# Where the output product stands between the gate and the val products of a fused attention and GLU kernel

## The chip, the cores and the metric

The kernel runs on one core of a Trainium2 chip. The metric is the time of one execution on the device, in microseconds (us). The core has five engines with a queue each: TensorE (PE in the profile) multiplies matrices, and its weight loads are a row of their own (PEld); VectorE (DVE), ScalarE (ACT) and GpSimd (POOL) work on elements; SyncE (SP) issues transfers. Each engine takes the instructions of its queue in the order in which the program lists them, and waits where an instruction needs what another engine has not finished.

## The reference

Two layers are fused. The first is a cross-covariance attention: for each of 4 batches, with q, k and v of 6016 rows and 256 channels,

```
s = kn.T @ qn / tau          # kn, qn: k and q scaled to length 1 down each column
a = softmax(s)               # 256 x 256
x = v @ a
```

The second is a gated linear unit on the 24064 rows of x, with 1536 hidden units:

```
gate = sigmoid(x @ w_gate)
out  = (gate * (x @ w_val)) @ w_out
```

## The kernel before, in words

The kernel never forms x. For each batch it multiplies the small matrix `a` with the weights, G = a @ w_gate and H = a @ w_val (function `gh`, 12 pieces a batch, each two matmuls of 512 columns and one store), and then needs only v: gate is v @ G, val is v @ H.

*Chunks and slots.* A batch is cut into 12 chunks of 512 rows (the last has 384), and a chunk into 12 slots `f`, one for each 128 hidden units. A slot is the unit in which everything is laid out. In it `glu` (line 655) makes one tile of the hidden layer:

- gate: two matmuls of 512 columns into `ps_gate`, then on ScalarE `g_sb` = tanh(gate/2) (line 676);
- val: two matmuls into `ps_val`;
- on VectorE `hT` = (tanh + 1) x val (line 677), in bf16. The missing factor 1/2 is carried in the scale with which H is stored.

`ps_gate` and `ps_val` have two buffers each, so a slot's val waits for the `hT` of two slots before.

*The output product.* hT @ w_out of a chunk runs during the next chunk. It is done with a scheme of seven block products in place of eight (the tables `PRODUCTS` and `ORDER`), so some of its operands are sums of blocks of hT. Those sums are made by `a_sum` on VectorE: the sum `m` = 0 (line 703, half the size), 1 (line 705) and 2 (line 707), each for two halves of the hidden units. The first half is done in the chunk itself, after the slots 7, 9 and 11 (`OWN_SLOTS`). The second half is done in the next chunk, after the slots 1, 3 and 5 (`NEXT_SLOTS`). `out_work` lists 84 matmuls of 128 columns for a chunk, and `run_work` takes one share of the list in each slot, seven of them (after the 384-row chunk the list is shorter, six in a slot, and sum 0 is first used in slot 2). By the order of the list, the second half of sum 0 is first used in slot 3 (by the first matmul of the share), that of sum 1 in slot 5 (the fifth), and that of sum 2 in slot 7 (the third). When a product of the list is complete, ScalarE copies it out of `ps_o` (`part`, line 756, and `whole`, line 763), and GpSimd adds the pieces (lines 757, 758, 773, 774).

*Side work.* The attention of batch b+1 is prepared during batch b: squares (ScalarE), sums for the scores (VectorE), score matmuls, and at the end of the batch the pieces of G and H. `side_work` writes a table of what follows each slot. The stores of G and H alternate between ScalarE (line 622) and VectorE (line 624). The pieces that do not fit any more go into `spill`, that is into the first slots of the next batch. In the last batch there is no such work.

*The order by hand.* The schedule is manual: the order in the program is the order in each queue. In a slot the main loop lists

```
glu(b, ci, f, ...)                # gate, val, tanh, hT
a_sum(...)                        # in the slots 1, 3, 5: for the chunk before
run_work(work, ...)               # the share of the output product
a_sum(...)                        # in the slots 7, 9, 11: for this chunk
for fn, a in spill + side: fn(*a) # scores, G/H, squares
```

`glu` has a parameter `between`, work that is listed between the gate's and the val's matmuls. Before the change only the very first chunk uses it, for pieces of G and H.

Of the kernel before, what the change touches and what calls it, by code (L numbers as in the profile page):

```python
# [9 lines left out]
FP32 = mybir.dt.float32  # L10
BF16 = mybir.dt.bfloat16
INT32 = mybir.dt.int32
ACT = mybir.ActivationFunctionType
# [36 lines left out]
def kernel(  # L50
# [20 lines left out]
    nc = tc.nc  # L71
    P = nc.NUM_PARTITIONS
# [9 lines left out]
    FC = DFF // P  # L82
# [3 lines left out]
    CH = TPC * P  # L86
# [11 lines left out]
    def pool(name, bufs, **kw):  # L98
        return ctx.enter_context(tc.tile_pool(name=name, bufs=bufs, **kw))
# [10 lines left out]
    gpool = pool("gpool", 3)  # L110
# [13 lines left out]
    def mm(out, lhsT, rhs, start, stop, **kw):  # L124
        nc.tensor.matmul(out, lhsT=lhsT, rhs=rhs, start=start, stop=stop, **kw)  # L125
# [74 lines left out]
    for f0, nf in pieces:  # L200
        if f0 + nf == DFF:
            load_v(0, 1)
        for w, src in enumerate((moe_w_gate, moe_w_val)):
            nc.gpsimd.dma_start(
                out=w_sb[w][f0 // FG][:, :, ds(f0 % FG, nf)],
                in_=src.rearrange("(t p) f -> p t f", p=P)[:, :, ds(f0, nf)],
# [5 lines left out]
    for n in range(FC // TPC):  # L212
        w_f32[n] = f32pool.tile([P, TPC, C], FP32, tag="f32", name="w_f32")
        nc.gpsimd.dma_start(
            out=w_f32[n], in_=moe_w_out.rearrange("(t p) c -> p t c", p=P)[:, n * TPC : (n + 1) * TPC, :]
# [412 lines left out]
    def gh(b, piece, pl, tag, act=None):  # L628
        gh_store(b, piece, gh_mms(b, piece, pl, tag), piece[3] == 0 if act is None else act)
# [25 lines left out]
    def glu(b, ci, f, between=None):  # L655
        t0, nt = groups[ci]
        n = nt * P
        G, H = st[b]["gh"]
        vT = vts[b, ci]
        if f == 0:  # L660
            hts[b, ci] = hpool.tile([P, FC, CH], BF16, tag="hT", name="hT")
        ps_gate = psg.tile([P, CH], FP32, tag="g", name="ps_gate")
        ps_val = psv.tile([P, CH], FP32, tag="v", name="ps_val")
        for ps, w in ((ps_gate, G), (ps_val, H)):
            for ib in range(CB):
                mm(
                    ps[:, :n],
                    w[f // (FG // P)][:, ib, ds(f % (FG // P) * P, P)],
                    vT[:, ib, :nt, :],
                    start=(ib == 0),  # L670
                    stop=(ib == CB - 1),
                )
            if between is not None and w is G:
                between()
        g_sb = gpool.tile([P, CH], FP32, tag="g", name="g_sb")
        nc.scalar.activation(out=g_sb[:, :n], in_=ps_gate[:, :n], func=ACT.Tanh, scale=0.5)  # L676
        nc.vector.scalar_tensor_tensor(  # L677
            out=hts[b, ci][:, f, :n],
            in0=g_sb[:, :n],
            scalar=1.0,  # L680
            in1=ps_val[:, :n],
            op0=ALU.add,
            op1=ALU.mult,
        )
# [3 lines left out]
    def a_sum(b, ci, g, m):  # L688

        nt = groups[ci][1]  # L690
        half = nt // 2
        hT = hts[b, ci]
        if (b, ci, g) not in sums:
            sums[b, ci, g] = spool.tile(
                [P, 5, FC // 4, CH // 2], BF16, tag=f"s{g}", name="sums", bufs=2 - g
            )
        f0, f1 = g * (FC // 2), (g + 1) * (FC // 2)
        n = half * P
        first, count = A_STEPS[m]
        out = sums[b, ci, g][:, first : first + count, :, :n].rearrange("p m j n -> p j m n")  # L700
        x = hT[:, f0:f1, : 2 * n].rearrange("p (j k) (r n) -> p j k r n", k=2, r=2)
        if m == 0:
            nc.vector.tensor_tensor(out=out[:, :, 0], in0=x[:, :, 0, 0], in1=x[:, :, 1, 1], op=ALU.add)  # L703
        elif m == 1:
            nc.vector.tensor_tensor(out=out, in0=x[:, :, 0], in1=x[:, :, 1], op=ALU.add)  # L705
        else:
            nc.vector.tensor_tensor(out=out, in0=x[:, :, :, 0], in1=x[:, :, :, 1], op=ALU.subtract)  # L707
# [94 lines left out]
    def run_work(work, share):  # L802

        upto = sum(w[0] for w in work) * share
        done = 0
        while work and done < upto:
            cost, fn, *args = work.pop(0)
            fn(*args)
            done += cost

    def store():
        while stores:
            b, ci = stores.pop(0)
            t0, nt = groups[ci]
            nc.sync.dma_start(out=out_rows[b][:, t0 : t0 + nt, :], in_=ffn.pop((b, ci))[:, :nt, :])
# [43 lines left out]
    for g, (t0, nt) in enumerate(groups0):  # L859
# [11 lines left out]
        while adds:  # L871
            w, last_sq = adds.pop()
# [55 lines left out]
    def side_work(b):  # L928
# [4 lines left out]
        def at(slot, fn, *a):  # L933
            side.setdefault(divmod(slot, FC), []).append((fn, a))
# [14 lines left out]
        n = b + 1  # L949
# [5 lines left out]
        for g, (t0, nt) in enumerate(groups if b == 0 else []):  # L955
            s0 = first + g * (last - first) // NCH
# [3 lines left out]
            for w in range(2):  # L960
                at(s0 + 1 + 4 * w, narrow_square, n, g, w)
                slot = s0 + 3 + 4 * w
                at(slot + slot % 2, narrow_add, n, g, w)
        step = (last - first) / len(wide)
        for g, (t0, nt) in enumerate(wide if b else []):
            s0 = first + int(g * step)
# [19 lines left out]
        s0 = 8 * FC + 2  # L986
# [27 lines left out]
        at(s0 + 28, all_sums, n)  # L1014
        at(s0 + 28, gh_tiles, n)
        for i, piece in enumerate(gh_order):
            slot = s0 + 30 + 2 * i
            if slot < NCH * FC:
                at(slot, gh, n, piece, *((pss, "s"), (psm, "m"))[i % 2])
            else:  # L1020
                spill.setdefault((n, *divmod(slot - NCH * FC, FC)), []).append((gh, (n, piece, psm, "m")))
# [8 lines left out]
    def gh_pieces(ns):  # L1030
        for n in ns:
            gh(0, gh_first[n], *gh_banks[n % 4])

    prev = None
    for b in range(B):
        side = side_work(b)
        for ci in range(NCH):
            final = (b, ci) == (B - 1, NCH - 1)
            for f in range(FC):
                mid = gh_mid.get(f) if (b, ci) == (0, 0) else None  # L1040
                glu(b, ci, f, None if mid is None else (lambda: gh_pieces(mid)))
                if prev is not None:
                    if f == 4:
                        store()
                    if f + final in NEXT_SLOTS and prev != (0, 0):
                        a_sum(*prev, 1, NEXT_SLOTS[f + final])
                    run_work(work, 1 / max(1, FC - final - f))
                if f in OWN_SLOTS and not final and (b, ci) != (0, 0):
                    a_sum(b, ci, 0, OWN_SLOTS[f])
                for fn, a in spill.get((b, ci, f), []) + side.get((ci, f), []):  # L1050
                    fn(*a)
                if (b, ci) == (0, 0):
                    gh_pieces(gh_end.get(f, ()))
            prev = (b, ci)
            if not final:
                work = out_work(*prev)
# [39 lines left out]
```

## Time and profile before

| | before |
|---|---|
| median of 3 runs | 805.0 us (803.94 to 805.98) |
| span of the profiled run | 803.2 us |
| granted TensorE clock, mean | 0.998 |
| TensorE busy | 779.8 us |
| VectorE busy | 688.5 us |
| ScalarE busy | 526.3 us |
| GpSimd busy | 443.6 us |
| tanh (line 676), 576 times | 588 ns each |
| hT (line 677), 576 times | 672 ns each |
| sums of the lines 703, 705 and 707, 92 times each | 546, 1102 and 1029 ns each |

How to read it: busy time is what an engine spent in instructions other than waits, and the rest of the span is what it stood idle. The mean of a group is over all its instructions, the smaller ones of the 384-row chunks too. The line of every matmul is that of a helper (L125), so matmuls are told apart by the names of their tiles: `ps_gate`, `ps_val`, `ps_o` (output product), `ps_s` (scores), `ps_gh` (G and H). In the timeline a line can stand for several instructions of a kind that follow each other (x7), and then the second number is from the start of the first to the end of the last. The end of a matmul is modelled, so the distance from start to start is what counts.

### The profile page before, as it was taken

How to read it: one execution, taken by the hardware profiler on the slowest of the kernel's cores; microseconds unless marked ns; L12 is line 12 of the kernel's file. 1: busy time of each engine (PE TensorE's matmuls, PEld its weight loads, DVE VectorE, ACT ScalarE, POOL GpSimd, SP SyncE). 2: the span in 40 equal slices, each digit the busy share in tenths (PEclk: the TensorE clock that was granted, in tenths of full speed). 3: DMA queues.
4: the chain of work that ended last, by engine and by line, in shares of the span. 5: the costliest groups of instructions: out<-in, count | busy, mean ns of one | idle time of the engine just before them, and what ended most of it. 6: DMA issues, size and time to landing. Idle time of an engine off the chain costs nothing.

```text
span 803.2 us, 18022 instructions
## 1 busy us (share of the span) xinstructions
PE 779.8 (97%) x6861; PEld 497.7 (62%) x6875; DVE 688.5 (86%) x1044; ACT 526.3 (66%) x891; POOL 443.6 (55%) x621
## 2 busy tenths in 40 slices
PE   3899999999999999999999999999999999999998
PEld 2556666666656666666665666666666566666666
DVE  5767989999878898889988889989987888888886
ACT  3766777766667767676667677766666565665664
POOL 3566565546454677565842755676754344444443
PEclk9999999999999999999999999999999999999999
DMA  9997759432676899863477599987234333432402
GB/s 214 203 199 127 131 97 139 89 66 54 137 146 132 165 173 191 172 123 53 103 138 155 109 172 179 186 152 137 51 71 80 60 66 65 82 67 64 88 29 73
DMA packets 82775, 95.15 MB, mean 118 GB/s; under 512 B 52512, under 2 KB 58528, under 8 KB 82688
## 3 DMA queue, kind: packets, MB, share of 16 engines
q0 software_dynamic: 25616, 55.85, 39.4%
q1 hardware_dynamic: 56496, 37.30, 21.6%
q8 instruction: 53, 0.87, 0.4%
q10 hardware_dynamic: 576, 0.85, 0.3%
q14 instruction: 34, 0.28, 0.1%
HBM read 79.04 MB, written 24.64 MB: 129 GB/s over the span
## 4 chain that ended last, share of the span: by engine, by line
PE 93%; DMA 4%; DVE 1%; issue 1%; ACT 1%; POOL 0%; DVEq 0%; ACTq 0%; POOLq 0%
PE ps_gate L125 30%; PE ps_val L125 30%; PE ps_o L125 27%; DMA qk_sb<-in_k_dram 4%; PE ps_s L125 4%; PE ps_gh L125 2%; DVE hT L677 0%; ACT acc L292 0%; DVE sums L703 0%; ACT g_sb L676 0%; PE ps_end L125 0%; DVE qs L354 0%; DVE sums L705 0%; DVE sums L707 0%; PE ps_n L125 0%
## 5 line engine op out<-in xcount | busy, mean ns | idle before, releaser
L676 ACT ACTIVATE g_sb<-ps_gate 128x512 f32<-128x512 f32 (+1 forms) x576 | 337.9, 588 | 224.5 <-PE ps_gate L125 204.7
L677 DVE SCALAR_TENSOR_TENSOR hT<-g_sb,ps_val 128x512 bf16<-128x512 f32 (+1 forms) x576 | 385.7, 672 | 95.5 <-ACT g_sb L676 77.5
L125 PE MATMUL ps_val<-vT,gh_H 128*128 128x512 bf16 (+1 forms) x1152 | 337.5, 375 | 1.4 <-DVE hT L677 1.4
L125 PE MATMUL ps_gate<-vT,gh_G 128*128 128x512 bf16 (+1 forms) x1152 | 337.6, 375 | 0.2
L125 PEld LDWEIGHTS <-sums 128*128 128x128 bf16 x2670 | 182.8, 98 | 85.2 <-DVE sums L703 3.9
L125 PEld LDWEIGHTS <-gh_H 128*128 128x128 bf16 x1152 | 112.7, 98 | 132.6 <-issue 2.4
L773 POOL TENSOR_TENSOR out_sb<-out_sb,m_sb 128x256 f32<-128x256 f32 x89 | 89.2, 1002 | 170.8 <-ACT out_sb L763 145.6
L125 PE MATMUL ps_o<-w_sums,sums 128*128 128x128 bf16 x1602 | 154.9, 219 | 2.0 <-DVE sums L703 1.9
L125 PEld LDWEIGHTS <-hT 128*128 128x128 bf16 x1200 | 88.2, 98 | 46.9
L757 POOL TENSOR_TENSOR m_sb<-m_sb 128x128 f32<-128x128 f32 x89 | 51.3, 576 | 98.5 <-ACT m_sb L756 98.3
L705 DVE TENSOR_TENSOR sums<-hT 128x1536 bf16<-128x1536 bf16 (+1 forms) x92 | 101.4, 1102 | 0.0
L125 PEld LDWEIGHTS <-gh_G 128*128 128x128 bf16 x1152 | 92.8, 98 | 12.5 <-DVE gh_G L624 0.3
L125 PE MATMUL ps_o<-w_out_sb,sums 128*128 128x128 bf16 x1068 | 96.3, 219 | 0.0
L125 PE MATMUL ps_o<-w_sums,hT 128*128 128x128 bf16 x1068 | 95.5, 219 | 0.0
L707 DVE TENSOR_TENSOR sums<-hT 128x1536 bf16<-128x1536 bf16 (+1 forms) x92 | 94.7, 1029 | 0.0
L758 POOL TENSOR_TENSOR m_sb<-m_sb 128x128 f32<-128x128 f32 x89 | 81.4, 914 | 7.0
L774 POOL TENSOR_TENSOR out_sb<-out_sb 128x256 f32<-128x256 f32 x89 | 78.4, 881 | 7.0
L763 ACT COPY out_sb<-ps_o 128x512 f32<-128x512 f32 x89 | 52.2, 587 | 11.4 <-PE ps_o L125 8.5
L703 DVE TENSOR_TENSOR sums<-hT 128x768 bf16<-128x768 bf16 (+1 forms) x92 | 50.3, 546 | 0.0
L125 PE MATMUL ps_s<-qk_sb 128*128 128x256 bf16 (+1 forms) x194 | 34.7, 297 | 15.4 <-DMA qk_sb<-in_k_dram 8.5
L756 ACT COPY m_sb<-ps_o 128x384 f32<-128x384 f32 x89 | 42.7, 479 | 6.5 <-PE ps_o L125 4.0
L252 ACT ACTIVATE sq<-qk_sb 128x1024 bf16<-128x1024 bf16 (+3 forms) x36 | 35.6, 1009 | 12.0 <-DMA qk_sb<-in_k_dram 11.9
(105 smaller groups left out, 510.0 us busy)
## 6 DMA issues: line engine op xcount, KB each, us to landing
out_dram<-out_sb SPq DMA_DIRECT2D x43, 512.0 KB, 3.4
v_sb<-in_v_dram POOLq DMA_DIRECT2D x44, 256.0 KB, 5.3
acc<-sq POOLq DMA_DIRECT2D x16, 512.0 KB, 7.0
qk_sb<-in_q_dram POOLq DMA_DIRECT2D x14, 512.0 KB, 10.3
qk_sb<-in_k_dram POOLq DMA_DIRECT2D x14, 512.0 KB, 8.2
qs<-qk_sb POOLq DMA_DIRECT2D x20, 256.0 KB, 5.5
qk_sb<-in_q_dram POOLq DMA_DIRECT2D x15, 256.0 KB, 5.6
qk_sb<-in_k_dram POOLq DMA_DIRECT2D x15, 256.0 KB, 6.3
```

The costliest lines, as they stand in the source:

```text
L125: nc.tensor.matmul(out, lhsT=lhsT, rhs=rhs, start=start, stop=stop, **kw)
L676: nc.scalar.activation(out=g_sb[:, :n], in_=ps_gate[:, :n], func=ACT.Tanh, scale=0.5)
L677: nc.vector.scalar_tensor_tensor(out=hts[b, ci][:, f, :n], in0=g_sb[:, :n], scalar=1.0, in1=ps_val[:, :n], op0=ALU.add, op1=ALU.mult,)
L703: nc.vector.tensor_tensor(out=out[:, :, 0], in0=x[:, :, 0, 0], in1=x[:, :, 1, 1], op=ALU.add)
L705: nc.vector.tensor_tensor(out=out, in0=x[:, :, 0], in1=x[:, :, 1], op=ALU.add)
L707: nc.vector.tensor_tensor(out=out, in0=x[:, :, :, 0], in1=x[:, :, :, 1], op=ALU.subtract)
L756: nc.scalar.copy(m, states[p]["ps"][:, : 3 * P].rearrange("p (n c) -> p n c", c=P))
L757: nc.gpsimd.tensor_tensor(out=m[:, 1, :], in0=m[:, 1, :], in1=m[:, 2, :], op=ALU.add)
L758: nc.gpsimd.tensor_tensor(out=m[:, 2, :], in0=m[:, 1, :], in1=m[:, 0, :], op=ALU.add)
L763: nc.scalar.copy(o[:, p : p + half + 1 : half, :], states[p]["ps"].rearrange("p (t c) -> p t c", c=C),)
L773: add(out=ends, in0=ends, in1=states[p]["m"][:, 1:3, :], op=ALU.add)
L774: add(out=ends, in0=ends, in1=mids, op=ALU.subtract)
```

## The change

The share of the output product moves from behind the hidden tile to between its gate and its val products. Tanh is listed ahead of that share, so that ScalarE can work on it while TensorE does output matmuls, and VectorE has both operands of hT when val is done. What stands behind the slot (the sums, the side work) keeps its place. The G/H pieces at the end of a batch move from even slots to the odd slots just before. The first chunk, which has no output product yet, keeps its G/H pieces between gate and val; there too tanh is now listed ahead of them.

```
@@ glu
         ps_val = psv.tile([P, CH], FP32, tag="v", name="ps_val")
+        g_sb = gpool.tile([P, CH], FP32, tag="g", name="g_sb")
         for ps, w in ((ps_gate, G), (ps_val, H)):
             for ib in range(CB):
                 mm(
...
-            if between is not None and w is G:
-                between()
-        g_sb = gpool.tile([P, CH], FP32, tag="g", name="g_sb")
-        nc.scalar.activation(out=g_sb[:, :n], in_=ps_gate[:, :n], func=ACT.Tanh, scale=0.5)
+            if w is G:
+                nc.scalar.activation(out=g_sb[:, :n], in_=ps_gate[:, :n], func=ACT.Tanh, scale=0.5)
+                if between is not None:
+                    between()
         nc.vector.scalar_tensor_tensor(
@@ side_work
         for i, piece in enumerate(gh_order):
-            slot = s0 + 30 + 2 * i
+            slot = s0 + 29 + 2 * i
@@ the main loop
                 mid = gh_mid.get(f) if (b, ci) == (0, 0) else None
-                glu(b, ci, f, None if mid is None else (lambda: gh_pieces(mid)))
+                if prev is not None:
+                    mid = lambda: run_work(work, 1 / max(1, FC - final - f))
+                elif mid is not None:
+                    mid = lambda ns=mid: gh_pieces(ns)
+                glu(b, ci, f, mid)
                 if prev is not None:
                     if f == 4:
                         store()
                     if f + final in NEXT_SLOTS and prev != (0, 0):
                         a_sum(*prev, 1, NEXT_SLOTS[f + final])
-                    run_work(work, 1 / max(1, FC - final - f))
```

## The prediction

> **What bounds the kernel now.** I read the page first: busy shares, slices, the chain that ended last.
>
> ```profile
> PE 779.8 (97%) x6861; PEld 497.7 (62%) x6875; DVE 688.5 (86%) x1044; ACT 526.3 (66%) x891; POOL 443.6 (55%) x621
> ...
> PE 93%; DMA 4%; DVE 1%; issue 1%; ACT 1%; POOL 0%; DVEq 0%; ACTq 0%; POOLq 0%
> ```
>
> TensorE is the bound: 93% of the chain. Its idle time is almost all in the first 37 us, which the change does not touch. So the question is what the change does to the few waits that TensorE has after that, and whether it makes new ones. The view of waits lists the old ones, and what VectorE waits for:
>
> ```profile
> DVE hT L677 <- ACT g_sb L676: 77.5, 161, 1.3
> PEld L125 <- DVE sums L703: 3.9, 7, 1.1
> PE ps_o L125 <- DVE sums L703: 1.9, 2, 1.0
> PE ps_val L125 <- DVE hT L677: 1.4, 3, 0.8
> ```
>
> Columns: total us, times, longest. VectorE waits 77.5 us for tanh, but it is not the bound. TensorE waits for VectorE for some 5 us in all: that is what can be won. Adding up, after 37 us, every gap between matmul starts that is longer than the matmul in front of it needs gives the same 5 us. Last I read the timeline of the last batch, where each chunk repeats the one before and no other work disturbs it (start, duration):
>
> ```profile
> 697.20 0.59 PE L125 MATMUL ps_gate<-vT,gh_G 128*128 128x512 bf16 x2
> 697.63 0.59 PE L125 MATMUL ps_val<-vT,gh_H 128*128 128x512 bf16 x2
> 697.83 0.60 ACT L676 ACTIVATE g_sb<-ps_gate 128x512 f32<-128x512 f32 x1 [0.66 <-PE ps_gate L125]
> 698.46 0.69 DVE L677 SCALAR_TENSOR_TENSOR hT<-g_sb,ps_val 128x512 bf16<-128x512 f32 x1 [0.57 <-ACT g_sb L676]
> 699.06 1.25 DVE L705 TENSOR_TENSOR sums<-hT 128x1536 bf16<-128x1536 bf16 x1
> ...
> 699.70 0.59 PE L125 MATMUL ps_gate<-vT,gh_G 128*128 128x512 bf16 x2
> ...
> 700.62 0.50 PE L125 MATMUL ps_o<-w_out_sb,sums 128*128 128x128 bf16 x6
> ...
> 701.57 1.13 DVE L707 TENSOR_TENSOR sums<-hT 128x1536 bf16<-128x1536 bf16 x1
> ...
> 703.08 0.55 PE L125 MATMUL ps_o<-w_sums,sums 128*128 128x128 bf16 x7
> ```
>
> This is slot 3 to slot 7 of a chunk. Gate and val take 0.43 us each (697.20, 697.63), seven output matmuls 0.39 us, a slot 1.25 us. The hT product waits for tanh, and starts 1.26 us after the gate. The sum of slot 3 ends at 700.31 and is first needed by the fourth of the six matmuls at 700.62, that is at 700.79 (0.056 each). The sum of slot 5 ends at 702.70 and is needed by the third of the seven at 703.08, that is at 703.19. What a wait costs at least is seen where one happened:
>
> ```profile
> 234.09 0.35 DVE L703 TENSOR_TENSOR sums<-hT 128x384 bf16<-128x384 bf16 x1
> ...
> 234.50 0.34 PE L125 MATMUL ps_o<-w_sums,sums 128*128 128x128 bf16 x3 [0.97 <-DVE sums L703]
> ```
>
> The sum ends at 234.44 and TensorE goes on at 234.50: 0.06 us. So the slack of the two sums above is 700.79 - 700.31 - 0.06 = 0.42 us and 703.19 - 702.70 - 0.06 = 0.43 us.
>
> **What the Trainium skill says.** "TensorE: Matmul & The Clock Gate", section "Wait — 56ns, not 53.3ns?", gives 55.6 ns and 215.7 ns from start to start for 128 and 512 columns; this trace has 56 and 215, so TensorE is at its rate, and an order of matmuls can only gain by removing waits. The same page, section "Architectural detail: the array is 16× 32×32, not 1× 128×128", says that TensorE may pull weight loads ahead of matmuls but that ScalarE and VectorE are strict queues. In this trace a weight load starts one matmul early and no more, so a load that waits for sums holds all that is behind it. "SBUF — State Buffer", section "SBUF: two separate sides", says VectorE and GpSimd exclude each other on a shared port for some operations. The trace fits in part: L705 takes 0.95 us in some chunks and 1.25 in the one above, where GpSimd's adds lie beside it.
>
> **The change, part by part.**
>
> *Output share between gate and val.* No matmul is added or removed. On TensorE the order "gate, val, output, side" becomes "gate, output, val, side". Two things follow. The output share of each slot comes 0.43 us (two matmuls of 0.215) sooner after its gate. And val comes 0.39 us later, so hT can start later. From gate to tanh the trace takes 0.63 us after the first of the two matmuls (697.20 to 697.83). Taking the same for val, hT starts at 0.43 + 0.39 + 0.63 = 1.45 us after its gate, where tanh let it start at 1.26: 0.19 us later. This is an estimate, as no hT in the trace waits for val alone; if VectorE starts sooner after val than ScalarE after gate it is less, and 0 at the least. So tanh is hidden, but the chain val, hT, sum now ends 0.19 us later while its user comes 0.43 us earlier. The slack falls by 0.62 us, or 0.43 at the least. Where hT was late anyway (tanh behind a copy or a square, or VectorE behind in its queue) it falls by 0.43 only.
>
> The wait stands in front of the weight load of an output matmul; behind it in the queue are the rest of the share and val, then hT of that slot. Nothing fills the gap. In the chunk above: the slot 3 sum 0.62 - 0.42 = 0.20 us, the slot 5 sum 0.62 - 0.43 = 0.19 us; the half-size sum of slot 1 has 0.89 us and stays hidden. 0.39 us for each such chunk. The gap does not help the second sum, since its own val and hT are behind the gap.
>
> The same subtraction for all three sums in all 46 chunks that have them, with each one's own slack and own start of hT:
> - ten equal chunks of the last batch: 10 x 0.39 = 3.9 us; the final one 0.3;
> - six chunks of the earlier batches like them (no score work): 1.3;
> - chunks with squares and score sums, where some sums are already late or nearly so (slack 0 to 0.4): 3.8. The chunks of the first batch with 256-wide scores have 0.6 to 0.7 and pay nothing;
> - the three chunks with most of the next batch's G/H: 1.1; the three at a batch's start: 1.3.
> Sum 11.7 us.
>
> *G/H one slot ahead.* The same 12 products with the same stores for each batch. In the chunk before a batch's end, a G/H store on ScalarE (0.65 us) now lies in slot 4, delays tanh of slot 5, and makes the slot 5 sum late. In slot 3 the store ends before tanh of slot 4 is due. So the 1.1 us goes. At the batch's start, a G/H product (0.43 us) now lies in slot 1, between the sum and its first user in slot 2, and the store of slot 0 moves back to slot 11: I take no extra there (-1.3) and 0.3 us less in two of the old waits of 0.97 to 1.1 us. On VectorE a store (0.7 us) now follows a sum in odd slots. hT of the next slot is then up to 0.8 us late, but val's buffer is asked for again two slots later, and no sum follows in the even slot. Nothing.
>
> *Val's own waits.* Val waits for hT of two slots before, 1.4 us in all. Val is 0.39 us later, so they shrink: -0.4 us, since in the other chunks the next sum decides anyway.
>
> *Tanh ahead of the G/H pieces in the first chunk.* TensorE is not waiting there: nothing. *Copies of finished outputs* come sooner in ScalarE's queue, before the next tanh is due; the buffer they free is needed after the same 0.43 + 0.43 + 0.33 us as now: nothing.
>
> GpSimd's adds start with the copy, some 0.27 us sooner, and overlap the slot 3 and 5 sums less: -0.5 us.
>
> Sum: 11.7 - 1.1 - 1.3 - 0.6 - 0.4 - 0.5 = 7.8, so **805 + 8 = 813 us**.
>
> **Rivals.**
> - *Sums are hardly late.* hT starts no later than now. Then the chunks of the last batch pay 0 to 0.01 us, and what is left is the 3.8 us of the score chunks less the savings: about 807 to 808. For: the 0.19 is an estimate. Against: val's matmuls must end first, and they end 0.39 us later. Chance 0.15.
> - *Faster.* The waits for VectorE fall away because tanh is out of hT's way. TensorE has 5 us of them: at most 800, and 802 if three in five go. For: 77.5 us of VectorE's waiting does go. Against: most of the 5 us are waits for sums, whose users come earlier. Chance 0.05; together with a draw near 805, 0.1.
> - *VectorE becomes the bound in odd slots with G/H.* A slot with hT 0.67, a sum 1.1 and a store 0.7 has 2.5 us of work in 1.25 to 1.7 us. If its delay reaches TensorE each time: 18 stores x 0.3 us = 5 us more, about 818. Against: the even slot after it has 0.7 only. Chance 0.1.
>
> **How the numbers follow.** The forecast case (811 to 816) has 0.65, the smaller one 0.15, the rival with VectorE 0.1, no change or faster 0.1. Range 806 to 818: the lower end is the case with no later hT, the upper the sum of 11.7 with nothing saved, and one us for waits that I do not see. Faster by over 0.3% 0.05, within 0.3% 0.07, slower 0.88.
>
> **What would show it.** In the profile after: hT's idle for tanh nearly gone, and hT waiting for val; waits of weight loads and output matmuls for the sums of L705 and L707 new, some 0.2 us each in slots 5 and 7 of every chunk of the last batch, which takes about 15.4 us for a chunk and not 15.05; TensorE's busy time the same. It would be wrong if hT still starts 1.26 us after its gate, if the last batch's chunks keep 15.05 us, or if the loss sits in chunks with G/H.

## The result, and the profile after

The changed kernel takes 808.9 us (median of 6 runs, 807.6 to 810.9), the kernel before 805.5 us in the same series (the 805.0 us of the table above is the median of the first three of its six runs): 1.0047 times as long, 95% interval 1.0027 to 1.0067. It is slower by 3.4 us, where 8 were forecast. The page after, in the lines that answer to those of before:

```profile
PE 783.3 (97%) x6861; PEld 497.1 (62%) x6875; DVE 682.6 (85%) x1044; ACT 513.4 (64%) x891; POOL 435.8 (54%) x621
...
PE 86%; DVE 6%; DMA 5%; issue 1%; ACT 1%; POOL 1%; DVEq 0%; ACTq 0%; POOLq 0%
```

TensorE is still the bound, but VectorE now has 6% of the chain that ended last, from 1%. ScalarE and VectorE are not busier. TensorE's busy time is 3.5 us longer for the same 6861 matmuls. Their ends are modelled: one of 128 columns stands with 0.22 us, though the next can start after 0.056, so a short wait between two of them is counted as busy. The view of waits (us in total, times, longest) says what VectorE and TensorE wait for:

```profile
DVE hT L678 <- PE ps_val L125: 85.4, 193, 0.8
DVE hT L678 <- ACT g_sb L675: 9.7, 17, 1.4
PEld L125 <- DVE sums L704: 9.4, 22, 1.3
PEld L125 <- DVE sums L708: 3.2, 11, 0.4
PE ps_o L125 <- DVE sums L704: 2.1, 5, 0.8
```

hT waits for val and hardly for tanh any more (9.7 us, 77.5 before); in all VectorE waits no less. The waits for the sums have grown, above all those for sum 0 (now line 704) and sum 2 (now 708), and the row of `ps_val` waiting for hT is gone.

The view of waits takes a weight load's wait for a wait, though the matmul behind it may still start in time. So I also added up, for each trace from 37 us on, all gaps of over 0.05 us between the starts of matmuls beyond what the matmul in front needs (gaps of just one 512-wide matmul beside G/H products, 13 in each of the traces before and after, are missing records and are left out). By what the matmul after the gap needed, in us:

| kernel | time, times that of before | waits for sums | val's waits for hT |
|---|---|---|---|
| before | 1 | 2.9 | 2.0 |
| changed | 1.0047 | 8.1 | 0 |
| changed, G/H back in even slots | 1.0090 | 11.4 | 0.3 |
| before, G/H ahead | 0.9974 | 0.5 | 1.6 |
| changed, sums a slot sooner | 1.0003 | 0.5 | 4.6 |
| changed, sum ahead of hT | 0.9983 | 1.5 | 1.1 |
| changed, share split 3 and 4 | 0.9999 | 4.4 | 0.9 |
| before, G/H ahead, sum ahead of hT | 1.0054 | 0 | 9.5 |
| before, G/H ahead, sums a slot sooner | 1.0040 | 0 | 7.9 |

The two columns account for the times: in each row their sum differs from that of the first row by what the ratio says, to within 0.9 us, so no more than that is left for a cost of the order itself. (With G/H back in even slots the profiled run also waited 1.1 us, once, for a transfer of weights at 44 us; that is in neither column.) From before to after these gaps grow by 3.3 us and the smaller ones by 0.6; the profiled spans are 803.2 and 807.1 us. By place, the waits for sums grew from 0.3 to 5.1 us in the chunks with score work (below: score chunks), from 0 to 0.9 in ten chunks of the last batch, from 0 to 0.5 in the final one and from 0 to 0.4 in the six earlier chunks without score work; at the three batch starts they fell from 2.5 to 1.1.

### The profile page after: what moved, and what is told of

The parts are those of the page before. It is cut to its first block, busy times and chain, and to the rows that moved or that the text cites. A ratio compares the mean times of both kernels' runs of the same rounds, so it can differ in the third digit from the quotient of the medians.

```text
span 807.1 us, 18022 instructions
## 1 busy us (share of the span) xinstructions
PE 783.3 (97%) x6861; PEld 497.1 (62%) x6875; DVE 682.6 (85%) x1044; ACT 513.4 (64%) x891; POOL 435.8 (54%) x621
## 4 chain that ended last, share of the span: by engine, by line
PE 86%; DVE 6%; DMA 5%; issue 1%; ACT 1%; POOL 1%; DVEq 0%; ACTq 0%; POOLq 0%
PE ps_val L125 28%; PE ps_gate L125 27%; PE ps_o L125 25%; DMA qk_sb<-in_k_dram 4%; DVE hT L678 3%; PE ps_s L125 3%; PE ps_gh L125 2%; DVE sums L708 1%; DMA v_sb<-in_v_dram 1%; DVE sums L704 0%; DVE sums L706 0%; POOL out_sb L775 0%; ACT g_sb L675 0%; DVE qs L359 0%; POOL out_sb L774 0%
## 5 line engine op out<-in xcount | busy, mean ns | idle before, releaser
L678 DVE SCALAR_TENSOR_TENSOR hT<-g_sb,ps_val 128x512 bf16<-128x512 f32 (+1 forms) x576 | 385.8, 671 | 105.3 <-PE ps_val L125 85.4
L125 PE MATMUL ps_o<-w_sums,sums 128*128 128x128 bf16 x1602 | 158.2, 219 | 3.6 <-DVE sums L704 2.1
L774 POOL TENSOR_TENSOR out_sb<-out_sb,m_sb 128x256 f32<-128x256 f32 x89 | 67.6, 760 | 173.1 <-ACT out_sb L764 149.5
L125 PEld LDWEIGHTS <-gh_G 128*128 128x128 bf16 x1152 | 104.2, 98 | 82.2 <-DVE gh_G L624 0.3
L758 POOL TENSOR_TENSOR m_sb<-m_sb 128x128 f32<-128x128 f32 x89 | 43.6, 490 | 112.9 <-ACT m_sb L757 112.6
L775 POOL TENSOR_TENSOR out_sb<-out_sb 128x256 f32<-128x256 f32 x89 | 94.8, 1065 | 7.0
L708 DVE TENSOR_TENSOR sums<-hT 128x1536 bf16<-128x1536 bf16 (+1 forms) x92 | 98.5, 1071 | 0.0
L125 PEld LDWEIGHTS <-gh_H 128*128 128x128 bf16 x1152 | 90.2, 98 | 3.3 <-DVE gh_H L624 0.3
L759 POOL TENSOR_TENSOR m_sb<-m_sb 128x128 f32<-128x128 f32 x89 | 85.9, 965 | 7.0
L706 DVE TENSOR_TENSOR sums<-hT 128x1536 bf16<-128x1536 bf16 (+1 forms) x92 | 88.6, 963 | 0.0
L125 PEld LDWEIGHTS <-qk_sb 128*128 128x128 bf16 x286 | 29.7, 104 | 43.3 <-issue 10.1
```

Source lines behind the costliest of these rows:

```text
L678: nc.vector.scalar_tensor_tensor(out=hts[b, ci][:, f, :n], in0=g_sb[:, :n], scalar=1.0, in1=ps_val[:, :n], op0=ALU.add, op1=ALU.mult,)
L758: nc.gpsimd.tensor_tensor(out=m[:, 1, :], in0=m[:, 1, :], in1=m[:, 2, :], op=ALU.add)
L759: nc.gpsimd.tensor_tensor(out=m[:, 2, :], in0=m[:, 1, :], in1=m[:, 0, :], op=ALU.add)
L774: add(out=ends, in0=ends, in1=states[p]["m"][:, 1:3, :], op=ALU.add)
L775: add(out=ends, in0=ends, in1=mids, op=ALU.subtract)
```

## The experiments

**G/H apart from the share.** The first run undoes the G/H move, the second makes it alone:

```
-            slot = s0 + 29 + 2 * i
+            slot = s0 + 30 + 2 * i
```

> The changed kernel with the G/H pieces back in their even slots. Theory S (the loss is TensorE's waits for the second-half sums, whose users come sooner): moving G/H ahead was a help, since in the changed kernel the waits at the three batch starts are 0.43, 0.43 and 0.25 us against 1.14, 1.14 and 0.19 before; without it they return, so 1 to 2 us more than the changed kernel, 809.5 to 811. Rival G (the G/H pieces in odd slots, stored by VectorE behind a sum, are the loss): 3 us less, 806 or below.

> The kernel before with the G/H pieces one slot ahead and nothing else. Theory S: the waits of 1.14 us at two batch starts shrink by the G/H product (0.43 us) that now lies between the sum and its user, so 0.5 to 1.5 us less than before, 804 to 805. Rival G: 2 to 3 us more than before, 807 to 808.5.

Measured: 812.0 us against 805.0 for the kernel before (1.0090, interval 1.0075 to 1.0105), and 802.8 us (0.9974, 0.9965 to 0.9982). G/H in odd slots is a gain in both orders, 3.5 us in the changed kernel and 2.1 in the one before, by the ratios. Both went theory S's way and further than it said, by about 1 us each. Rival G is out. Moving the share alone costs 7.0 us. Where G/H helps is at the start of a batch. TensorE there, in the run with G/H back:

```profile
233.78 0.33 PE L125 MATMUL ps_o<-w_sums,sums 128*128 128x128 bf16 x3
235.51 0.34 PE L125 MATMUL ps_o<-w_sums,sums 128*128 128x128 bf16 x3 [1.41 <-DVE sums L704]
```

and in the changed kernel, where a G/H piece stands in slot 1 (one of its two records is missing):

```profile
232.53 0.38 PE L125 MATMUL ps_gh<-w_gate,e_sb 128*128 128x512 bf16 x1
...
233.18 0.33 PE L125 MATMUL ps_o<-w_sums,sums 128*128 128x128 bf16 x3
233.77 0.34 PE L125 MATMUL ps_o<-w_sums,sums 128*128 128x128 bf16 x3 [0.26 <-DVE sums L704]
```

The distance between the two groups falls from 1.73 to 0.59 us. That is more than the piece's 0.43, since the G/H store (0.69 us) is also out of ScalarE's queue in slot 0, where tanh of slot 1 stood behind it and a square. At the three batch starts the waits are 3.8 us with G/H back and 1.1 us in the changed kernel.

**Are the waits for sums the loss?** Two runs give the sums more time and leave the share between gate and val. In one they come a slot sooner (all but the final chunk's, which were in the slots 0, 2 and 4 already, by the `+ final` that goes here), in the other in the same slot but ahead of hT in VectorE's queue:

```
-NEXT_SLOTS = {1: 0, 3: 1, 5: 2}
+NEXT_SLOTS = {0: 0, 2: 1, 4: 2}
...
-                    if f + final in NEXT_SLOTS and prev != (0, 0):
-                        a_sum(*prev, 1, NEXT_SLOTS[f + final])
+                    if f in NEXT_SLOTS and prev != (0, 0):
+                        a_sum(*prev, 1, NEXT_SLOTS[f])
```

```
+                if prev is not None and f + final in NEXT_SLOTS and prev != (0, 0):
+                    a_sum(*prev, 1, NEXT_SLOTS[f + final])
                 glu(b, ci, f, mid)
...
-                    if f + final in NEXT_SLOTS and prev != (0, 0):
-                        a_sum(*prev, 1, NEXT_SLOTS[f + final])
```

> The changed kernel with the second-half sums after the slots 0, 2 and 4 in place of 1, 3 and 5, so each has a slot (1.25 us) more until its user. Theory S: the 8.1 us of waits for sums in the changed kernel go, but for some in the chunks with score sums, which lie in the slots 0, 4 and 8 too: 801 to 804, below the kernel before. Rival V (the loss is that hT waits for val, so VectorE is held back in every slot, or that the order of matmuls itself costs): no gain, 807 to 810.

> The changed kernel with each second-half sum still in the slot 1, 3 or 5, but listed ahead of that slot's hT on VectorE, so it can run while hT would wait for val. The sum is ready some 0.7 to 1.3 us sooner, hT of that slot up to 0.7 us later. Theory S: waits for sums go nearly everywhere, 801 to 804. Rival V: hT is later still, so 810 or more.

Measured: 805.1 us (1.0003, 0.9996 to 1.0011) and 803.5 us (0.9983, 0.9976 to 0.9989). Both take back the whole loss, the second more, so the waits for sums are the loss. But the first is 1.1 us above theory S's range: its waits for sums are gone but for the final chunk's 0.5 us, and 4.6 us of val waiting for hT have come. The sums now share the slots 0 and 4 with score sums, and 3.8 of the 4.6 us lie in the chunks with score work.

**Is the place of the share worth anything by itself?** The same two edits on the kernel before, with G/H ahead:

> The kernel before (share behind val) with the G/H pieces one slot ahead and the second-half sums listed ahead of hT. Against the run with the share between and the same sums (803.5 us) only the place of the share differs. Theory S: once the sums are in time the place is worth nothing: within 1.5 us of it, 802 to 804. Rival V: the place between costs some us by itself, so this one is 2 us or more faster, 801.5 or below.

> The kernel before (share behind val) with the G/H pieces one slot ahead and the second-half sums after the slots 0, 2 and 4. Compared with the G/H move alone (802.8 us). Theory S: the sums were in time nearly everywhere there, so nothing is left to gain in waits for sums (0.4 us), and score sums in slots 0 and 4 now meet them and delay hT, for which val waits: 802.5 to 804.5. Rival: with a slot more for every sum the remaining 2 us of waits go, 801 to 802.

Measured: 809.1 us (1.0054, 1.0037 to 1.0070) and 808.2 us (1.0040, 1.0026 to 1.0054). All the expectations missed; the last theory S had the mechanism (hT delayed, val waiting), but not its size. What helps the changed kernel hurts the other by 5 to 6 us over the G/H move alone. No wait for a sum is left in these two, and val waits 9.5 and 7.9 us for hT, where it is 1.6 with the G/H move alone. One of them in the run with the sum ahead of hT:

```profile
305.61 1.20 DVE L707 TENSOR_TENSOR sums<-hT 128x1536 bf16<-128x1536 bf16 x1
...
306.73 1.27 DVE L677 SCALAR_TENSOR_TENSOR hT<-g_sb,ps_val 128x512 bf16<-128x512 f32 x2
...
307.46 0.59 PE L125 MATMUL ps_val<-vT,gh_H 128*128 128x512 bf16 x2 [0.34 <-DVE hT L677]
```

The sum holds hT until 306.73, the first hT ends about 307.4, and val starts at 307.46. So VectorE's queue has two deadlines on TensorE: the sums for the share, and hT for the val of two slots later. The share between gate and val gives val's deadline 0.39 us more and takes from the sums'. With the share behind val it is the other way round. In these runs neither place is better by itself: each with the order on VectorE that suited it best, they come out alike (0.9983 and 0.9974, with intervals that overlap).

**Is it val's shift or the share's?** The change makes val later by 0.39 us and the share sooner by 0.43. The share split, three matmuls between and four behind val (`take_work`, which is new, takes a slot's share off the list), leaves 0.17 of the first:

```
-                    mid = lambda: run_work(work, 1 / max(1, FC - final - f))
+                    taken = take_work(work, 1 / max(1, FC - final - f))
+                    mid = lambda: run_work(taken, 3 / 7)
...
                         a_sum(*prev, 1, NEXT_SLOTS[f + final])
+                    run_work(taken, 1)
```

> The changed kernel with three of the seven output matmuls between gate and val, and four behind val and the sum as before. Val is then 0.17 us later and not 0.39, so hT can start 1.26 us after its gate, as before. The user of the slot 3 sum is the fifth matmul and so stays behind val; those of the sums of slots 1 and 5, the first and the third, still come 0.43 us sooner. Theory S (slack): no waits in the last batch (the slot 5 sum has 0.43 - 0.43 and what it gains by being shorter), few in the score chunks: 802.5 to 805. Rival V (work between gate and val costs by itself, three sevenths of the 7 us that the share costs with G/H back in place): 805.5 to 807.

Measured: 804.9 us (0.9999, 0.9988 to 1.0010), at the upper end of theory S. hT waits for tanh again (73.9 us, and 12.9 for val), and in the ten chunks of the last batch no wait is left: there the loss needed val's shift. Of the 4.4 us of waits for sums 3.6 lie in score chunks. It is 2 us slower than the kernel before with the G/H move alone, so the sooner share still costs where sums are late anyway.

**Why the last batch paid so little.** In the forecast each of its chunks loses 0.39 us, in slots 5 and 7; it lost 0.087, all in slot 7. The timeline of the changed kernel there, slots 3 to 7:

```profile
700.00 0.59 PE L125 MATMUL ps_gate<-vT,gh_G 128*128 128x512 bf16 x2
700.82 0.59 PE L125 MATMUL ps_val<-vT,gh_H 128*128 128x512 bf16 x2
701.52 0.69 DVE L678 SCALAR_TENSOR_TENSOR hT<-g_sb,ps_val 128x512 bf16<-128x512 f32 x1 [0.57 <-PE ps_val L125]
701.69 0.45 POOL L758 TENSOR_TENSOR m_sb<-m_sb 128x128 f32<-128x128 f32 x1 [2.28 <-ACT m_sb L757]
702.13 0.95 DVE L706 TENSOR_TENSOR sums<-hT 128x1536 bf16<-128x1536 bf16 x1
702.21 1.18 POOL L759 TENSOR_TENSOR m_sb<-m_sb 128x128 f32<-128x128 f32 x1
702.99 0.50 PE L125 MATMUL ps_o<-w_out_sb,sums 128*128 128x128 bf16 x6
704.64 0.95 DVE L708 TENSOR_TENSOR sums<-hT 128x1536 bf16<-128x1536 bf16 x1
705.45 0.65 PE L125 MATMUL ps_o<-w_sums,sums 128*128 128x128 bf16 x7
```

hT starts 1.52 us after its gate: 0.26 later than before, not 0.19. But the sums take 0.95 us, where they took 1.25 and 1.13. The wait is inside the last line, which takes 0.65 us for seven matmuls and took 0.55 before. GpSimd's adds in the kernel before, beside the sum that ran from 699.06 to 700.31:

```profile
699.05 0.44 POOL L757 TENSOR_TENSOR m_sb<-m_sb 128x128 f32<-128x128 f32 x1 [2.15 <-ACT m_sb L756]
699.57 1.05 POOL L758 TENSOR_TENSOR m_sb<-m_sb 128x128 f32<-128x128 f32 x1
```

Before, an add was at work when the sum would start, and the sum was the longer one. Now the first add ends as the sum starts, the sum goes through, and the second add is stretched to 1.18 us. Two runs leave the adds out:

```
-            add(out=ends, in0=ends, in1=states[p]["m"][:, 1:3, :], op=ALU.add)
-            add(out=ends, in0=ends, in1=mids, op=ALU.subtract)
```

and likewise the two adds of `part`.

> The kernel before without GpSimd's four adds of each output tile (its output rows are left without the sums of the block products). Theory L (the sums of the slots 3 and 5 took 1.25 and 1.13 us because GpSimd's adds lay beside them): in the last batch both take 0.95 us, and the slacks grow from 0.42 and 0.43 to 0.72 and 0.61 us. Rival: the durations are the sums' own, and stay 1.25 and 1.13. The time in both cases within 1 us of before, as these sums are in time there.

> The changed kernel without the same adds. Theory L: the sums of the slots 3 and 5 take 0.95 us with and without the adds, since in the changed kernel the sum is at work when the second add would start; the waits of 0.087 us in slot 7 of the last batch stay, and the time falls by less than 2 us, for sums elsewhere that still met adds. Rival: the sums get shorter than 0.95 and the waits in slot 7 go.

Measured, one run each: 804.1 us for the kernel before without adds, 805.5 for the changed one. The sums of the slots 3 and 5 in the last batch of the first:

```profile
697.74 0.95 DVE L705 TENSOR_TENSOR sums<-hT 128x1536 bf16<-128x1536 bf16 x1
...
700.25 0.95 DVE L707 TENSOR_TENSOR sums<-hT 128x1536 bf16<-128x1536 bf16 x1
```

0.95 us, as theory L has it, and the same in the second. There the waits of 0.086 us in slot 7 of the last batch stay. But the changed kernel falls by some 3 us and not by under 2: its waits for sums go from 8.1 to 4.6 us, and of the 5.1 us in score chunks at most 0.2 is left. So GpSimd is in two parts of the result: out of the sums' way in the last batch, and still in it in the score chunks. Both runs also have one long wait for a sum near 385 us that the others don't have (1.0 and 1.7 us), and GpSimd is in that too: the sum takes 2.55 us, beside adds of the attention (line 430) that GpSimd works off in a row, and it ends 0.8 us after the last of them. With the output's adds in front of them, as in the run with the G/H move alone, these adds begin 0.05 us after the same sum, and it takes 0.95.

Then I tried to put GpSimd back in the way, with one more instruction ahead of the adds of `part`; first a multiplication by 1:

```
+            nc.gpsimd.tensor_scalar(out=m[:, 1:3, :], in0=m[:, 1:3, :], scalar1=1.0, scalar2=None, op0=ALU.mult)
             nc.gpsimd.tensor_tensor(out=m[:, 1, :], in0=m[:, 1, :], in1=m[:, 2, :], op=ALU.add)
```

> The changed kernel with one more GpSimd instruction ahead of the two adds that follow the copy of a finished part: a multiplication by 1 in place, 128x256. It begins with the copy's end, some 0.45 us ahead of the sums of slots 3 and 5, and should last 0.6 to 0.9 us, so GpSimd is at work when each of these sums would start, as it was before the change. Theory L (the forecast of 8 us was too high because the sums got out of the adds' way): in the last batch the sums of slots 3 and 5 take 1.15 to 1.3 us in place of 0.95, waits of 0.2 to 0.35 us appear in slots 5 and 7, 0.4 to 0.6 us more for a chunk there, and 811.5 to 816 in all. Rival (where the sum starts decides nothing; they are shorter for another reason): sums of 0.95 us and 808 to 809.5.

Measured: 809.7 us (1.0069, 1.0048 to 1.0089), sums of 0.95 us. The numbers are the rival's, though the multiplication did lie over the sum's start:

```profile
702.35 0.84 POOL L758 TENSOR_SCALAR m_sb<-m_sb 128x256 f32<-128x256 f32 x1 [2.24 <-ACT m_sb L757]
...
702.78 0.95 DVE L706 TENSOR_TENSOR sums<-hT 128x1536 bf16<-128x1536 bf16 x1
```

This instruction, with one operand, does not hold the sum; 65 sums of this size in the trace begin while it is at work, and 63 of them take 0.95 to 0.96 us. So the next had two, the adds' own kind:

```
+            nc.gpsimd.tensor_tensor(
+                out=m[:, 1:3, :],
+                in0=m[:, 1:3, :],
+                in1=nought.rearrange("p (j o) -> p j o", o=1).to_broadcast([P, 2, P]),
+                op=ALU.add,
+            )
```

> As the run with the multiplication by 1, but the additional GpSimd instruction is an add with two operands (a zero spread over 128x256), as the adds of the kernel are. The multiplication, with one operand, lay over the start of both sums for 0.84 us and they still took 0.95 us. Theory L2 (two instructions with two operands each, one on VectorE and one on GpSimd, shut each other out, and the one that begins first goes through): now the sums of slots 3 and 5 in the last batch take 1.15 to 1.35 us, waits of 0.15 to 0.35 us come in slots 5 and 7, and the whole takes 811.5 to 816 us. Rival: sums of 0.95 us again, 808 to 810.

Measured: 813.0 us (1.0103, 1.0078 to 1.0128), in theory L2's range, but not in its way: the add with a spread zero took only 0.60 us and ended as the sum started, so that nine of the ten chunks have sums of 0.96 to 0.98 us and waits of 0.09 to 0.10. The tenth chunk shows the other case. There hT came late, and an add was at work when the sum began:

```profile
719.93 0.46 POOL L766 TENSOR_TENSOR m_sb<-m_sb 128x128 f32<-128x128 f32 x1
...
720.04 1.16 DVE L708 TENSOR_TENSOR sums<-hT 128x1536 bf16<-128x1536 bf16 x1
```

The add kept its 0.46 us and the sum took 1.16. In the neighbours the sum keeps its time and the add takes 1.06. That is theory L2 in one chunk; as an experiment on the last batch's time this run is inconclusive, and what it added lies mostly in score chunks.

The rule behind it stands on all the traces together, the thirteen runs of this document. They have 671 sums of 128x1536 that take over 1.00 us. In 645 of them a two-operand instruction of GpSimd ends 0.82 us before the sum does, to within 0.02: the sum is held until that one, or a row of them without a pause, is through.

## Why the prediction was right, and where its sizes were off

The direction, the range (806 to 818) and the mechanism came out. The forecast case (811 to 816) did not, and the loss is 3.4 us and not 8. Of the signs it named, hT waits for val and no longer for tanh, and the waits for sums are there; but slot 5 of the last batch has none, slot 7 has 0.087 us and not 0.2, a chunk there takes 15.15 us and not 15.4, and TensorE's busy time is not the same. By term, forecast and measured:

- *"The question is what the change does to the few waits"; the wait for sums is the new one.* Right, and shown by the two runs that give the sums more time and win the loss back.
- *hT 0.19 us later.* 0.26. The tanh wait is gone, as forecast.
- *Ten chunks of the last batch, 3.9 us.* This is the term that was mis-sized most: 0.9 measured. The step was "GpSimd's adds ... overlap the slot 3 and 5 sums less: -0.5 us". That took part of the overlap off; but the one that starts first goes through. The sums lost all of the 0.30 and 0.18 us. With those and 0.26, the forecast's own subtraction gives 0.43 + 0.26 - 0.42 - 0.30 = -0.03 for slot 3, no wait, and 0.43 + 0.26 - 0.43 - 0.18 = 0.08 for slot 5, where 0.087 was measured.
- *Six earlier chunks like them, 1.3 us.* 0.4, in three of the six, and again for the sum of slot 5 alone.
- *Score chunks, 3.8 us.* The waits for sums there grew by 4.8; without the adds nearly all of them are gone.
- *G/H: three of the 11.7 us saved.* 3.5 us measured, but most of it at the batch starts (2.7); the chunks with most of G/H would have paid 0.3 and not 1.1.
- *Val's own waits, -0.4 us.* -2.0: all of them went. In the chunk with the longest, 0.98 us, a wait of 0.95 us for a sum came in its place.
- *Rivals.* The rival of later G/H stores on VectorE is out. "Sums are hardly late" (807 to 808) came nearest in time, but not by its reason, that hT starts no later: hT is later, and the sums are shorter.
- *The sum, 7.8 us.* In the traces: last batch 0.9, final chunk 0.5, six chunks 0.4, score chunks 4.8, batch starts -1.4, val -2.0, gaps too small to name 0.6. That is 3.8, and the spans differ by 3.9. The errors went both ways, so that the total is inside the range is in part luck. What stays open is the 0.6 us.

## What to carry to other kernels

Before moving work between two stages of a full engine, list every deadline that another engine's queue has on it, and take the shift from each slack: here one order gave 0.39 us to val and took 0.69 from the sums. A move that hides a wait of an engine that is not the bound (77.5 us of VectorE waiting for tanh) gained nothing by it here, as hT now waits 85.4 us for val; what counts is which result the full engine needs next. Durations in a trace hold for their neighbours only: shift a queue by 0.26 us, as here, and an instruction that was held up by another engine may run free, or the reverse. Here two versions are faster than both kernels: the share left behind val and the G/H pieces alone moved, 802.8 us (0.9974), and the share between with the sums ahead of hT, 803.5 us (0.9983). Their intervals overlap.

## What the runs showed of the hardware

A VectorE sum of two bf16 operands (128x1536) takes 0.95 us with GpSimd free, or with a two-operand add of GpSimd that starts after it, which is then stretched from 0.46 us to between 1.05 and 1.18. Where such an add is at work when the sum would start, the sum is longer (1.25 and 1.13 us in the last batch before the change) and ends 0.82 us after the add. The Trainium skill, "SBUF — State Buffer", section "SBUF: two separate sides", says that the port pair that the two share is locked for a whole instruction by the one that starts first, and not divided; the traces agree for these adds. The same place counts every GpSimd operation that reads this memory against a VectorE operation with two inputs there. Here the measurement differs: a GpSimd multiplication by a constant, which reads one operand from it, lay over the start of the sum for 0.4 us and did not lengthen it. Why it doesn't was not tested.
